# Two chained layers behind clustered attention: the sums and the output products of a step are queued one step later

## The chip, the cores and the metric

The kernel runs on one core of one Trainium2 chip. The metric is the device time of one execution in microseconds (us). The engines named below are PE (matrix products), DVE (vector), ACT (activation), POOL (GpSimd) and SP (which issues the transfers). Each takes its instructions in the order in which they were written for it, and they wait for each other through semaphores.

## The reference

Clustered attention gives 1536 rows of 512 numbers. Two layers follow, and the change lies in them:

```python
def _moe_ref(x, w_in, w_out):                  # first layer, 512 -> 2048 -> 512
    h = x @ w_in
    g = np.maximum(0.01 * h, h)
    return g @ w_out

def _moe2_ref(x, w_in, w_out, a, b):           # second layer, same sizes
    h = x @ w_in
    P = a[0] + a[1] * h + a[2] * h * h + a[3] * h * h * h
    Q = 1.0 + np.abs(b[0]) * np.abs(h) + np.abs(b[1]) * h * h
    g = P / (Q + 1e-06)
    return g @ w_out
```

## The kernel before

**Steps.** Both layers are cut into 112 steps. A step takes one block of tokens (512 in the first layer, 384 in the second) and one slice of 128 of the 2048 hidden numbers. Steps 0 to 47 are the first layer, 48 to 111 the second. Every matrix is split into a high and a low part (names that end in h and l), and a product is three products. PE's part of step i is 12 matmuls for h(i) and then, once the nonlinearity is there, 12 (first layer) or 9 (second) for y(i). The steps of one token block and one group of slices add up in the same y tiles; a group has 4 slices, but the first group of the first layer is cut into two of 2. At the last slice the y tiles are added to an array in SBUF, by three or four DVE operations named acc (`collect`). I call that **the sums of step s** and the change to the next y tiles a **crossing**. There are as many sums of a crossing as y tiles, and each y tile has a single buffer, so that y(s+1), the first of the next block, cannot start in a tile before that tile's sum is done.

**Between h and y.** In the first layer ACT applies the leaky step to h (L1064), ACT casts gh (L1055) and DVE takes gl = h - gh (L1060). In the second layer ACT makes |h| as y (L1071) and u (L1072), POOL makes z in two operations (L1075, L1078), DVE two operations on u (L1079, L1080), ACT the reciprocal r by ln and exp (L1091, L1092), DVE three operations that end in g, written over h (L1093, L1096, L1099), then gh and gl as before. h has four buffers in PSUM.

**Order.** The scheduler is off: what the last loop of the program writes in pass i is the order on every engine. In pass i PE gets h(i) and then y(i-3) (`LAG = 3`); gh and gl have three buffers each. So gh(i) also waits for y(i-3), which reads the buffer that it takes over.

**Weights.** Among these operations stand those that fetch and split the weights of later groups (`weights.step`, the last thing in each pass). In the first layer the weights come as 64-bit numbers and are converted: ACT L818, DVE L825 and L831, then an ACT cast (L838) and a POOL subtraction (L841). In the second layer only the last two are left, one pair in every second step of its first three groups.

Of the kernel before, what the change touches and what calls it, by code (L numbers as in the profile page):

```python
# [30 lines left out]
def clustered_attention_moe_moe2(  # L31
# [103 lines left out]
    def tile_of(x):  # L135
        u, a = divmod(x, T // 2)
        return a * 2 + u

    class Attention:
# [414 lines left out]
        def hi(self, u, part):  # L554
            un = self.unit[u]
            gi, i = divmod(u, QT)
            if i == 0 and part == 0:
                self.group[gi] = {
                    "ph": self.pt.tile([P, T, BLK], F32R, tag="ph", name="ph"),
                    "pl": self.pt.tile([P, T, BLK], F32R, tag="pl", name="pl"),  # L560
                }
            n = T // 2
            un["hi", part] = self.group[gi]["ph"][:, part * n:(part + 1) * n, i * P:(i + 1) * P]
            nc.scalar.copy(un["hi", part], un["pT", part])  # L564

        def lo(self, u, part):
            un = self.unit[u]
            gi, i = divmod(u, QT)
            n = T // 2
            nc.vector.tensor_tensor(  # L570
                self.group[gi]["pl"][:, part * n:(part + 1) * n, i * P:(i + 1) * P],
                un["pT", part], f32(un["hi", part]), op=ALU.subtract,
            )
            if part == 1:
                del self.unit[u]
# [349 lines left out]
    def queue_group(n):  # L925
        for which in ("wi", "wo"):
            if (n, which) in scratch:
                weights.add((which, n), scratch[n, which], which, n % 2, False)
            else:
                weights.add((which, n), weight_source(n, which), which, n % 2, WIDE)  # L930
# [10 lines left out]
    with tc.manual_schedule():  # L941
        wctx = ctx.enter_context(ExitStack())
# [49 lines left out]
        yp = wctx.enter_context(tc.tile_pool(name="yp", bufs=1))  # L992
        x1["c"] = [yp.tile([P, NCT, BLK], F32R, name=nm) for nm in ("xhc", "xlc")]
        accs = yp.tile([P, NCT * NT], F32, name="acc")
        gp_ = wctx.enter_context(tc.tile_pool(name="gp", bufs=3))
        ew = wctx.enter_context(tc.tile_pool(name="ew", bufs=2))
        open_stage("wstb")
        hps = wctx.enter_context(tc.tile_pool(name="hps", bufs=4, space=PSUM))
# [3 lines left out]
            weights.step()  # L1002

        LNC = float(2.0 ** -LN_SHIFT)
        LAG = 3
        steps = [
            (n, j, f) for n, (m, f0, nf) in enumerate(groups)
            for j in range(NT // width(m)) for f in range(nf)
# [2 lines left out]
        NS = len(steps)  # L1011
        st = {}
        cur = {}

        def mm3(o, pairs, first, last):
            n = len(pairs)
            for idx, (l, r) in enumerate(pairs):
                nc.tensor.matmul(  # L1018
                    o, lhsT=l, rhs=r,
                    start=(first and idx == 0), stop=(last and idx == n - 1),  # L1020
                )

        def tl(nm):
            return ew.tile([P, BLK], F32, tag=nm, name=nm)

        def rational(i):
            return groups[steps[i][0]][0] == 1

        def wide(i):
            return width(groups[steps[i][0]][0])  # L1030
# [31 lines left out]
        def leaky(i):  # L1062
            h = st[i]["h"]
            nc.scalar.activation(h, h, AF.Prelu, alpha=0.01)  # L1064
            hi(i)
            lo(i)

        def ratio_act(i):
            d = st[i]
            d["y"], d["z"], d["u"] = tl("y"), tl("z"), tl("u")  # L1070
            nc.scalar.activation(d["y"], d["h"], AF.Abs)  # L1071
            nc.scalar.activation(  # L1072
                d["u"], d["h"], AF.Identity, bias=nav[:, 2:3], scale=nav[:, 3:4]
            )
            nc.gpsimd.tensor_scalar(  # L1075
                d["z"], d["y"], abv[:, 1:2], abv[:, 0:1], op0=ALU.mult, op1=ALU.add
            )
            nc.gpsimd.tensor_tensor(d["z"], d["z"], d["y"], op=ALU.mult)  # L1078
            nc.vector.tensor_tensor(d["u"], d["u"], d["h"], op=ALU.mult)  # L1079
            nc.vector.scalar_tensor_tensor(  # L1080
                d["u"], d["u"], nav[:, 1:2], d["h"], op0=ALU.add, op1=ALU.mult
            )

        def ratio_end(i):
            d = st[i]
            if i < M0 + LAG:
                r = tl("r")
            else:
                r = yps.tile([P, 512], F32, tag="y3", name="r")[:, 0:BLK]
            ln = tl("ln")  # L1090
            nc.scalar.activation(ln, d["z"], AF.Ln, scale=LNC, bias=lnc)  # L1091
            nc.scalar.activation(r, ln, AF.Exp, bias=lnb, scale=-1.0)  # L1092
            nc.vector.scalar_tensor_tensor(  # L1093
                d["u"], d["u"], nav[:, 0:1], r, op0=ALU.add, op1=ALU.mult
            )
            nc.vector.scalar_tensor_tensor(  # L1096
                r, d["z"], 1.000001, r, op0=ALU.add, op1=ALU.mult
            )
            nc.vector.scalar_tensor_tensor(  # L1099
                d["h"], r, -2.0, d["u"], op0=ALU.add, op1=ALU.mult  # L1100
            )

        def start(i):
            if rational(i):
                ratio_act(i)
            else:
                leaky(i)

        def shape(i):
            final = rational(i)  # L1110
            return final, QT if final else NCT, 512

        def back(i):
            n, j, f = steps[i]
            final, NO, NW = shape(i)
            d = st.pop(i)
            gh, gl = d["gh"], d["gl"]
            woh, wol = weights.get(("wo", n))
            for o in range(NO):
                if f == 0:  # L1120
                    cur[o] = yps.tile([P, 512], F32, tag=f"y{o}", name=f"y{o}")
                sl = slice(o * P, (o + 1) * P)
                if final:
                    pairs = [(gh[:, sl], woh[:, f, :]), (gh[:, sl], wol[:, f, :]), (gl[:, sl], woh[:, f, :])]
                else:
                    pairs = [(woh[:, f, sl], gh), (woh[:, f, sl], gl), (wol[:, f, sl], gh)]
                mm3(cur[o][:, 0:NW], pairs, f == 0, f == groups[n][2] - 1)

        def collect(i):
            n, j, f = steps[i]  # L1130
            first = groups[n][1] == 0
            nf = groups[n][2]
            last = groups[n][1] + nf == NG * NF
            final, NO, NW = shape(i)
            if f < nf - 1:
                return
            for o in range(NO):
                a = accs[:, (j * NO + o) * NW:(j * NO + o + 1) * NW]
                if first:
                    nc.vector.tensor_copy(a, cur[o][:, 0:NW])  # L1140
                else:
                    nc.vector.tensor_tensor(a, cur[o][:, 0:NW], a, op=ALU.add)
                if last:
                    if final:
                        b, t = divmod(j * QT + o, T)
                        t = tile_of(t)
                        nc.sync.dma_start(
                            out=out[b * S:(b + 1) * S, :].rearrange("(p t) c -> t p c", t=T)[t],
                            in_=a,
                        )  # L1150
                    else:
                        later.append((j, o, a))
# [9 lines left out]
                    nc.gpsimd.tensor_tensor(l, a[:, b - t0:e - t0], f32(h), op=ALU.subtract)  # L1162

        later = []
        for i in range(NS + LAG):
            if i < NS and steps[i][1:] == (0, 0):
                n1 = steps[i][0] + 1
                begin, total = i, 0
                count = NT // wide(i) * groups[n1 - 1][2]
                if n1 < len(groups):  # L1170
                    queue_group(n1)
                    if WIDE and n1 + NG - 1 > NG0 and n1 + NG - 1 < len(groups):
                        queue_scratch(n1 + NG - 1)
                    total = weights.pending()
            if i < NS:
                make_h(i)
            if i >= LAG:
                back(i - LAG)
            if 0 <= i - 1 < NS:
                start(i - 1)  # L1180
            if 0 <= i - 2 < NS and rational(i - 2):
                hi(i - 2)
                lo(i - 2)
            if later:
                next_x()
            if i >= LAG:
                collect(i - LAG)
            if 0 <= i - 1 < NS and rational(i - 1):
                ratio_end(i - 1)
            due = total * min(i - begin + 1, count - 1) // (count - 1)  # L1190
            weights.step(max(0, due - (total - weights.pending())))
            if i < LAG and weights.waits_for(("wo", 0)):
                weights.step(4)
            if i == LAG - 2:
                while weights.waits_for(("wo", 0)):
                    weights.step()
# [29 lines left out]
```

## Time and profile before

| what | value |
|---|---|
| median of 3 runs | 810.77 us (810.54 to 816.19) |
| the profiled execution, its own time | 810.76 us |
| its span in the trace | 808.9 us |
| PE busy | 790.3 us, 98% of the span |
| DVE, ACT, POOL busy | 655.8, 526.7, 401.5 us |
| first layer, first h to the second layer's first h | 269.29 to 524.82 us |
| second layer, first h to the last sum | 524.82 to 805.81 us |

Matmuls are pipelined, so the busy time of PE says little about small waits. They are seen in the starts: 12 matmuls of a step that start at equal distances are not held up, and a longer distance is a wait.

### The profile page before, as it was taken

The page shows a single profiled execution, that of the slowest core. Times are in us where ns is not written, and L with a number is a line of the kernel's source. Part 1 is how long each engine was busy: PE and PEld are TensorE (multiplying, and loading weights), DVE is VectorE, ACT ScalarE, POOL GpSimd, SP SyncE. Part 2 cuts the span into 40 slices and gives each one's busy share as a digit, 9 for nine tenths or more (in the row PEclk, how much of TensorE's full clock was granted, in tenths as well). Part 3 has the DMA queues.
Part 4 walks back from the last instruction along what each step waited for, and adds up shares of the span by engine and source line. Part 5 has one row for each costly group of instructions (what it writes and reads, how often), then busy time and mean ns, then how long its engine had stood idle before and what let it go on. Part 6 is the DMA issues. An engine that isn't in the chain of part 4 may idle for free.

```text
span 808.9 us, 12601 instructions
## 1 busy us (share of the span) xinstructions
PE 790.3 (98%) x4202; PEld 687.6 (85%) x4202; DVE 655.8 (81%) x1198; ACT 526.7 (65%) x1104; POOL 401.5 (50%) x440
## 2 busy tenths in 40 slices
PE   8899999999999999999999999999999999999997
PEld 5799898999888888888888888899989888988995
DVE  6788998988988678866577478668888888888997
ACT  4689988988899454453344245456676667766763
POOL 3867877877676323230031033267555555554442
PEclk9899999999999999999999999999999999999999
DMA  3783663753420224345446434421001010000112
GB/s 108 179 210 77 154 150 69 183 138 79 98 90 0 105 105 156 104 157 182 145 141 209 149 116 145 158 69 39 28 28 39 27 40 28 27 0 1 40 40 79
DMA packets 42256, 78.71 MB, mean 97 GB/s; under 512 B 5328, under 2 KB 25296, under 8 KB 42192
## 3 DMA queue, kind: packets, MB, share of 16 engines
q1 hardware_dynamic: 41904, 77.83, 32.7%
q8 instruction: 33, 0.54, 0.3%
q14 instruction: 31, 0.25, 0.1%
q10 hardware_dynamic: 288, 0.08, 0.0%
HBM read 49.84 MB, written 9.96 MB: 74 GB/s over the span
## 4 chain that ended last, share of the span: by engine, by line
PE 59%; POOL 14%; DVE 11%; ACT 9%; issue 7%; DMA 0%; POOLq 0%; DVEq 0%; ACTq 0%
PE h L1018 21%; PE y L1018 19%; POOL z L1078 5%; PE o L587 5%; PE s L507 5%; PE pT L551 5%; POOL z L1075 3%; DVE pl L570 3%; DVE nm L516 2%; PE sims L315 2%; POOL wol L841 2%; ACT ln L1091 2%; ACT r L1092 2%; POOL wil L841 2%; ACT ph L564 1%
## 5 line engine op out<-in xcount | busy, mean ns | idle before, releaser
L841 POOL TENSOR_TENSOR wil<-wf,wih 128x512 fp32r<-128x512 f32 x32 | 42.8, 1349 | 148.9 <-ACT wih L838 137.3
L570 DVE TENSOR_TENSOR pl<-pT,ph 128x384 fp32r<-128x384 f32 x192 | 97.2, 546 | 19.6 <-ACT ph L564 19.1
L1055 ACT CAST gh<-h 128x384 fp32r<-128x384 f32 (+1 forms) x112 | 59.0, 526 | 82.5 <-DVE h L1099 51.9
L543 POOL TENSOR_SCALAR e<-e,sum 128x768 f32<-128x768 f32 x96 | 87.9, 928 | 46.0 <-DVE sum L539 31.3
L1060 DVE TENSOR_TENSOR gl<-h,gh 128x384 fp32r<-128x384 f32 (+1 forms) x112 | 68.1, 608 | 40.7 <-ACT gh L1055 40.6
L564 ACT CAST ph<-pT 128x384 fp32r<-128x384 f32 x192 | 82.4, 481 | 17.1 <-PE pT L551 15.5
L1018 PE MATMUL h<-xha,wil 128*128 128x512 f32 (+1 forms) x256 | 93.5, 365 | 0.0
L1018 PE MATMUL h<-xha,wih 128*128 128x512 f32 (+1 forms) x256 | 93.3, 364 | 0.0
L1018 PE MATMUL h<-xla,wih 128*128 128x512 f32 (+1 forms) x256 | 93.3, 364 | 0.0
L516 DVE TENSOR_REDUCE nm<-s 128x1 f32<-128x768 f32 x96 | 90.8, 947 | 2.3 <-PE s L507 1.8
L527 ACT ACTIVATE e<-s,nm 128x768 f32<-128x768 f32 x96 | 87.3, 910 | 5.1 <-DVE sum L539 2.6
L551 PE MATMUL pT<-ident,e 128*128 128x128 f32 x576 | 82.7, 278 | 2.9 <-DVE pl L570 2.6
L831 DVE SCALAR_TENSOR_TENSOR wf<-st,wf 128x512 int32<-128x512 int32 x124 | 82.5, 717 | 0.0
L1075 POOL TENSOR_SCALAR z<-y,abv 128x384 f32<-128x384 f32 x64 | 43.1, 673 | 73.0 <-ACT y L1071 73.0
L1018 PE MATMUL y<-woh,gl 128*128 128x512 f32 x192 | 76.3, 398 | 0.7 <-DVE gl L1060 0.3
L1018 PE MATMUL y<-woh,gh 128*128 128x512 f32 x192 | 76.2, 397 | 0.8 <-ACT gh L1055 0.6
L551 PEld LDWEIGHTS pT<-ident,e 128*128 128x128 f32 x576 | 68.2, 144 | 9.4 <-DVE pl L570 3.6
L1018 PE MATMUL y<-wol,gh 128*128 128x512 f32 x192 | 75.2, 392 | 0.0
L1018 PE MATMUL y<-gh,wol 128*128 128x512 f32 x192 | 75.0, 390 | 0.0
L1018 PE MATMUL y<-gh,woh 128*128 128x512 f32 x192 | 74.8, 390 | 0.0
L1018 PE MATMUL y<-gl,woh 128*128 128x512 f32 x192 | 74.7, 389 | 0.0
L841 POOL TENSOR_TENSOR wol<-wf,woh 128x512 fp32r<-128x512 f32 x32 | 41.8, 1314 | 66.1 <-ACT woh L838 50.2
(125 smaller groups left out, 2044.3 us busy)
## 6 DMA issues: line engine op xcount, KB each, us to landing
st<-in_moe_w_out_dram SPq DMA_DIRECT2D x32, 512.0 KB, 4.4
st<-in_moe_w_in_dram SPq DMA_DIRECT2D x30, 512.0 KB, 4.6
a<-hl SPq DMA_DIRECT2D x56, 192.0 KB, 3.7
b<-hl SPq DMA_DIRECT2D x28, 192.0 KB, 5.9
wf<-scratch_wi SPq DMA_DIRECT2D x14, 256.0 KB, 2.6
qraw<-in_q_dram SPq DMA_DIRECT2D x16, 192.0 KB, 2.7
kraw<-in_k_dram SPq DMA_DIRECT2D x16, 192.0 KB, 3.6
vraw<-in_v_dram SPq DMA_DIRECT2D x8, 384.0 KB, 5.8
```

What stands on the lines that cost most here:

```text
L516: nc.vector.reduce_max(un["nm"], un["s"][:, 0:S], axis=AX.X, negate=True)
L527: nc.scalar.activation(un["e"], un["s"][:, 0:S], AF.Exp, bias=un["nm"], accum_out=un["recip"])
L543: nc.gpsimd.tensor_scalar(un["e"], un["e"], un["recip"], 1.0, op0=ALU.mult, op1=ALU.mult)
L551: nc.tensor.transpose(pp[:, kt * P:(kt + 1) * P], un["e"][:, k0:k0 + P], ident)
L564: nc.scalar.copy(un["hi", part], un["pT", part])
L570: nc.vector.tensor_tensor(self.group[gi]["pl"][:, part * n:(part + 1) * n, i * P:(i + 1) * P], un["pT", part], f32(un["hi", part]), op=ALU ...
L831: nc.vector.scalar_tensor_tensor(wi, hold["st", i][:, :, :, 1 - w], sc, wi, op0=op, op1=ALU.bitwise_or)
L841: nc.gpsimd.tensor_tensor(hold["l"][:, i:i + wr, :], hold["wf", i], f32(hold["h"][:, i:i + wr, :]), op=ALU.subtract,)
L1018: nc.tensor.matmul(o, lhsT=l, rhs=r, start=(first and idx == 0), stop=(last and idx == n - 1),)
L1055: nc.scalar.copy(d["gh"], d["h"])
L1060: nc.vector.tensor_tensor(d["gl"], d["h"], f32(d["gh"]), op=ALU.subtract)
L1075: nc.gpsimd.tensor_scalar(d["z"], d["y"], abv[:, 1:2], abv[:, 0:1], op0=ALU.mult, op1=ALU.add)
```

## The change

In pass i the order becomes: h(i); in the second layer ln and exp of step i-2; the first operations of step i-1; the three DVE operations that end step i-2; the two DVE operations on u of step i-1; the sums of step i-5; gh and gl of step i-2; a piece of the next layer's x if one is due; y(i-4); the weights. LAG is 4 in both layers, gh and gl get a fourth buffer, and `ratio_end` is split in three functions.

```diff
-        gp_ = wctx.enter_context(tc.tile_pool(name="gp", bufs=3))
+        gp_ = wctx.enter_context(tc.tile_pool(name="gp", bufs=4))
...
-        LAG = 3
+        LAG = 4
...
+        def ratio_poly(i):
+            d = st[i]
             nc.vector.tensor_tensor(d["u"], d["u"], d["h"], op=ALU.mult)
...
-        def ratio_end(i):
+        def ratio_recip(i):
             d = st[i]
             if i < M0 + LAG:
                 r = tl("r")
...
+            d["r"] = r
+
+        def ratio_end(i):
+            d = st[i]
+            r = d["r"]
...
-        for i in range(NS + LAG):
+        for i in range(NS + LAG + 1):
...
+            old = 0 <= i - 2 < NS and rational(i - 2)
+            new = 0 <= i - 1 < NS and rational(i - 1)
             if i < NS:
                 make_h(i)
-            if i >= LAG:
-                back(i - LAG)
-            if 0 <= i - 1 < NS:
-                start(i - 1)
-            if 0 <= i - 2 < NS and rational(i - 2):
+            if old:
+                ratio_recip(i - 2)
+            if new:
+                ratio_act(i - 1)
+            elif 0 <= i - 1 < NS:
+                leaky(i - 1)
+            if old:
+                ratio_end(i - 2)
+            if new:
+                ratio_poly(i - 1)
+            if i > LAG:
+                collect(i - LAG - 1)
+            if old:
                 hi(i - 2)
                 lo(i - 2)
             if later:
                 next_x()
-            if i >= LAG:
-                collect(i - LAG)
-            if 0 <= i - 1 < NS and rational(i - 1):
-                ratio_end(i - 1)
+            if LAG <= i < NS + LAG:
+                back(i - LAG)
```

On DVE in the first layer, around gl of steps 8 and 9, the order before, from the sums of step 5 on (acc; the gl rows are those of steps 8 and 9, the wf rows weight conversion):

```order
L1140 COPY acc<-y_4245 128x512
L1140 COPY acc<-y_4249 128x512
L1140 COPY acc<-y_4253 128x512
L1140 COPY acc<-y_4257 128x512
L831 SCALAR_TENSOR_TENSOR wf<-st,wf 128x512 x2
L825 TENSOR_SCALAR wf<-wf 128x512 x2
L1060 TENSOR_TENSOR gl<-h,gh 128x512
L831 SCALAR_TENSOR_TENSOR wf<-st,wf 128x512 x4
L1060 TENSOR_TENSOR gl<-h,gh 128x512
```

The same place after, with the same sums of step 5 at its end:

```order
L831 SCALAR_TENSOR_TENSOR wf<-st,wf 128x512 x2
L825 TENSOR_SCALAR wf<-wf 128x512 x2
L1060 TENSOR_TENSOR gl<-h,gh 128x512
L831 SCALAR_TENSOR_TENSOR wf<-st,wf 128x512 x4
L1060 TENSOR_TENSOR gl<-h,gh 128x512
L1142 COPY acc<-y_4286 128x512
L1142 COPY acc<-y_4290 128x512
L1142 COPY acc<-y_4294 128x512
L1142 COPY acc<-y_4298 128x512
```

The sums of step s stood behind gl(s+2) and now stand behind gl(s+4), and so behind two steps of weight conversion more.

On ACT in the second layer, at a step with a weight cast (L838), before:

```order
L1055 CAST gh<-h 128x384
L1091 ACTIVATE ln<-z,lnc 128x384
L1092 ACTIVATE r<-ln,lnb 128x384
L838 CAST woh<-wf 128x512
L1071 ACTIVATE y<-h 128x384
L1072 ACTIVATE u<-h,nav 128x384
```

and after:

```order
L1055 CAST gh<-h 128x384
L838 CAST woh<-wf 128x512
L1094 ACTIVATE ln<-z,lnc 128x384
L1095 ACTIVATE r<-ln,lnb 128x384
L1071 ACTIVATE y<-h 128x384
L1072 ACTIVATE u<-h,nav 128x384
```

Apart from the cast, ACT's order in the second layer is the same: what moved to the front of a pass stood at the end of the pass before.

On DVE at the end of the program, after:

```order
L1082 TENSOR_TENSOR u<-u,h 128x384
L1083 SCALAR_TENSOR_TENSOR u<-u,nav,h 128x384
L1144 TENSOR_TENSOR acc<-y_8813,acc 128x512
L1144 TENSOR_TENSOR acc<-y_8817,acc 128x512
L1144 TENSOR_TENSOR acc<-y_8821,acc 128x512
L1060 TENSOR_TENSOR gl<-h,gh 128x384
```

The first two rows are of step 111, the last step, and the sums are those of step 107; before, these sums stood two steps earlier, between gl of step 108 and the end operations of step 109.

## Rows read from the trace of the kernel before

**Rows 1.** The page, granted clock of PE in 40 slices (9 is 90% or more).

```profile
PEclk9899999999999999999999999999999999999999
```

**Rows 2.** Timeline of PE, second layer, first matmuls of h (start, length, instruction).

```profile
543.61 0.33 PE L1018 MATMUL h<-xha,wih 128*128 128x384 f32 x1
...
551.98 0.33 PE L1018 MATMUL h<-xha,wih 128*128 128x384 f32 x1
...
581.29 0.33 PE L1018 MATMUL h<-xhc,wih 128*128 128x384 f32 x1
...
729.61 0.34 PE L1018 MATMUL h<-xha,wih 128*128 128x384 f32 x1
...
746.69 0.34 PE L1018 MATMUL h<-xha,wih 128*128 128x384 f32 x1
...
775.90 0.34 PE L1018 MATMUL h<-xhb,wih 128*128 128x384 f32 x1
```

**Rows 3.** Timeline of PE, second layer, two neighbours in y.

```profile
600.49 0.39 PE L1018 MATMUL y<-wol,gh 128*128 128x512 f32 x1
601.00 0.50 PE L1018 MATMUL y<-woh,gl 128*128 128x512 f32 x1
```

**Rows 4.** Timeline of DVE, second layer, the first end operation of three steps.

```profile
579.36 0.61 DVE L1093 SCALAR_TENSOR_TENSOR u<-u,nav,r 128x384 f32<-128x384 f32 x1 [0.28 <-ACT r L1092]
...
584.29 0.61 DVE L1093 SCALAR_TENSOR_TENSOR u<-u,nav,r 128x384 f32<-128x384 f32 x1 [1.68 <-ACT r L1092]
...
587.84 0.61 DVE L1093 SCALAR_TENSOR_TENSOR u<-u,nav,r 128x384 f32<-128x384 f32 x1 [0.29 <-ACT r L1092]
```

**Rows 5.** Timeline of ACT, the ln in between (in brackets: idle before, releaser).

```profile
583.02 0.62 ACT L1091 ACTIVATE ln<-z,lnc 128x384 f32<-128x384 f32 x1 [1.47 <-POOL z L1078]
```

**Rows 6.** Timeline of POOL, same place.

```profile
579.94 1.30 POOL L841 TENSOR_TENSOR wol<-wf,woh 128x512 fp32r<-128x512 f32 x1 [1.89 <-ACT woh L838]
581.23 0.66 POOL L1075 TENSOR_SCALAR z<-y,abv 128x384 f32<-128x384 f32 x1
```

**Rows 7.** Timeline of PE, first layer: first y(0), then first matmuls of h(46), h(47).

```profile
280.48 0.39 PE L1018 MATMUL y<-gh,woh 128*128 128x512 f32 x1
...
513.78 0.39 PE L1018 MATMUL h<-xhb,wih 128*128 128x512 f32 x1
...
519.30 0.39 PE L1018 MATMUL h<-xhb,wih 128*128 128x512 f32 x1
```

**Rows 8.** Timeline of ACT, first layer, gh of step 45.

```profile
514.03 0.59 ACT L1055 CAST gh<-h 128x512 fp32r<-128x512 f32 x1 [0.64 <-PE y L1018]
```

**Rows 9.** Timeline of DVE, first layer, in order of time.

```profile
288.81 2.47 DVE L1140 COPY acc<-y 128x512 f32<-128x512 f32 x4
...
295.98 0.69 DVE L1060 TENSOR_TENSOR gl<-h,gh 128x512 fp32r<-128x512 f32 x1 [0.42 <-ACT gh L1055]
...
311.39 1.28 DVE L831 SCALAR_TENSOR_TENSOR wf<-st,wf 128x512 int32<-128x512 int32 x2
...
321.65 0.69 DVE L1060 TENSOR_TENSOR gl<-h,gh 128x512 fp32r<-128x512 f32 x1 [2.83 <-ACT gh L1055]
...
344.30 2.49 DVE L831 SCALAR_TENSOR_TENSOR wf<-st,wf 128x512 int32<-128x512 int32 x4
...
354.01 0.69 DVE L1060 TENSOR_TENSOR gl<-h,gh 128x512 fp32r<-128x512 f32 x1 [1.20 <-ACT gh L1055]
...
514.65 0.69 DVE L1060 TENSOR_TENSOR gl<-h,gh 128x512 fp32r<-128x512 f32 x1 [0.86 <-ACT gh L1055]
```

**Rows 10.** Timeline of PE at the end: first matmul of y(107).

```profile
790.51 0.40 PE L1018 MATMUL y<-woh,gh 128*128 128x512 f32 x1
```

**Rows 11.** Timeline of ACT at the end: u of step 110.

```profile
791.10 0.67 ACT L1072 ACTIVATE u<-h,nav 128x384 f32<-128x384 f32 x1
```

**Rows 12.** Timeline of DVE at the end: sums of steps 107 and 111.

```profile
791.41 2.08 DVE L1142 TENSOR_TENSOR acc<-y,acc 128x512 f32<-128x512 f32 x3 [0.99 <-PE y L1018]
...
803.73 2.08 DVE L1142 TENSOR_TENSOR acc<-y,acc 128x512 f32<-128x512 f32 x3 [0.59 <-PE y L1018]
```

More of the change, by code (lines that the diff above doesn't have):

```diff
@@ L1101, in ratio_end @@
             )
[L1103 to L1107, printed above, removed]
         def shape(i):
```

## The prediction

> **What bounds the kernel now.** I read the clock first, then the starts of PE's matmuls, then who is late where they are late. PE's clock is granted in full nearly everywhere [rows 1], so no time lies there. In the second layer PE's starts are even for long stretches: from h(100) at 746.69 to h(107) at 775.90 a step takes 4.173 us, and from h(54) to h(61) 4.187 [rows 2], both without a visible gap. A whole layer at that pace has nothing to give but its waits. Between h(52) at 543.61 and h(96) at 729.61, the stretch with weight casts, 44 steps take 186.0 us [rows 2], where 28 steps at 4.187 and 16 at 4.173 (the two paces alternate by group) would take 184.0. So **2.0 us** are waits. One of them is seen: two neighbours in y start 0.51 apart, and the second reads gl [rows 3]; nine of them in half a step would be 0.23 apart.
>
> Why gl is late shows on DVE. From one end operation to the next it takes 3.55 us without a weight cast and 4.93 with one [rows 4]; every second step has one, so the chain of gh, ln, exp and end operations goes at 4.24 us a step and PE at 4.18. The cast itself is not the price: its POOL subtraction takes 1.30, z starts as it ends, and ln then waits 1.47 for z [rows 5, 6]. The chain is slower than PE by 0.06 a step, uses up the three steps of room, and from then on PE waits.
>
> **Part 1, one more step of room in the second layer: -2.0 us.** y(i-4) instead of y(i-3) gives each gl one step of 4.18 us more. The shortfall over the 44 steps is 44 x 0.06 = 2.6 us, less than that, so the waits go even if the chain stays as slow. It won't: the cast now stands before ln, so POOL gets its 1.30 us while ACT does ln (0.62 [rows 5]), an exp of about that length and |h|, and z is not held up; I count this as nothing more, since the room already covers it. Bounds: 0 (the waits come back elsewhere) and -2.0 (there is no more to remove).
>
> **Part 2, the sums in the first layer: +3.4 us.** Here PE shows no wait now, so each new one is a full loss. A crossing after the change: PE has y(s), h(s+5), y(s+1). DVE has gl(s+4), the sums of s, more conversion. gh(s+4) takes over the buffer that y(s) reads, so it starts only when y(s) is through. What that costs is seen at step 45: PE starts the next h at 513.78, right behind the last matmul of y(42); gh waits for it and starts at 514.03, gl ends at 515.34 [rows 7 to 9], 1.56 after. A sum takes 0.68 and four take 2.47 [rows 9], so they start 0.60 apart; the first starts 0.08 before gl's end is recorded and ends at 2.16. PE wants y(s+1) after one h, half of the step of 5.52 [rows 7], or 2.76. So a crossing is free by 0.55 if DVE comes to gl in time.
>
> It doesn't at three of the fourteen crossings inside the layer, all in the first sixteen steps, where groups of two slices bring the sums every second step and two steps of conversion stand between.
> - Step 1. The order up to gl(3) is as before. Before, four sums took DVE from 288.81 and gl(5) ended at 296.67 [rows 9]; without them everything from there is 2.4 earlier, gl(5) ends at 294.27 and the first sum at 294.87. PE has h(4), y(0), h(5), y(1), h(6) from 280.48 [rows 7], 2.5 steps, and wants y(2) at 294.28. Wait **0.6**.
> - Step 5. The sums of step 3 end with the conversion starting 1.48 + 2.39 = 3.87 after y(3). From that first conversion to the end of gl(9) it was 311.39 to 322.34, 10.95 us [rows 9], the same operations as now. First sum ends at 3.87 + 10.95 + 0.60 = 15.42; PE wants y(6) at 13.80. Wait **1.6**.
> - Step 11. The same with 344.30 to 354.70, 10.40 us [rows 9]: 14.87 against 13.80. Wait **1.1**.
>
> With 0.05 of signalling at each this is 3.4. At the other crossings the conversion between has four steps to fit in, and I take the 0.55 as kept. Bounds: 0 (the conversion runs faster, once the sums no longer stand idle before it) and +6.7 (the other eleven each miss by 0.3).
>
> A rule speaks against this part. The Trainium skill, Perfetto Trace Analysis, "Optimizing Tensor Performance", says that independent groups of matmuls should rotate through PSUM banks so that emptying one overlaps the matmuls of the next. The y tiles here don't rotate, and by the rule every crossing would be exposed, which is the second rival below; the trace of before has no PE wait at these crossings, because h stands between, so I go by the rows.
>
> **Part 3, the end: -0.9 us.** The last h is now followed by five y, not four, so it ends one y earlier, 2.09 us. Before, the last h ended one step after y(107) began, 790.51 + 4.17 = 794.68, and the last sum at 805.81 [rows 10, 12]: 11.13 later. After, from the end of h(111): u of step 111 is ready after 1.25 (at step 110, h ends where y(107) starts, 790.51, and u ends at 791.77 [rows 10, 11]), two DVE operations of 0.6 each (their like in [rows 4]) and the first sum of step 107, 0.68, follow, so y(108) starts at 3.1 where PE could have started it at 2.09: a wait of 1.0 that is new. Then y(108) to y(110) take 6.26, and from the start of a y to its last sum it is 2.98 (790.51 to 793.49 [rows 10, 12]). Together 12.34. Less 11.13, less 2.09: -0.9. The sums are through by 4.5 us and step 111 needs one more circle of the chain, 3.55 [rows 4]: 8.1, before y(111) starts at 9.4, so it is covered. Bounds: -1.9 without the new wait, 0 if DVE is a step late.
>
> **Parts at nothing.** The fourth gh and gl buffer costs space only. The first layer's sums are copied into the second layer's x one piece per step; the last piece of the first block comes behind gh(46), 0.25 after y(42), and with gh 0.6 [rows 8], a cast like it and a subtraction like the 1.30 of [rows 6] it is there at 2.8 of the 5.5 us that PE still has until h(48). If that cover went, the second layer would start late by what exceeds it. h(4) now follows h(3) directly and needs gl(0)'s buffer, which is free as y(0) starts. SP's list of transfers is in the same order, and the output goes out behind the last sum as before. One more r lies in SBUF instead of PSUM.
>
> **Sum.** 3.4 - 2.0 - 0.9 = +0.5 on the profiled execution's own 810.76, which stands 0.01 under the median of the runs: **811.3 us**.
>
> **Rivals.**
> 1. The late sums don't come: DVE is ahead, since it no longer stands waiting for y with the conversion behind it. For it: the sums used to hold up the conversion, and the chains of part 2 contain ACT steps that then start earlier. Against: the intervals that I took contain no such wait. Time: 810.76 - 2.9 = 807.9. Chance 0.29.
> 2. Slower: the sums hold up y at every crossing of the first layer, because gh(s+4), gl(s+4) and the first sum stand in a row behind y(s). It decides as soon as gl(s+4) ends later than 2.1 us after y(s). Price: 14 crossings at 1.4, the mean of 1.6 and 1.1, less the 2.9 gained: 810.76 + 19.6 - 2.9 = 827.5. For it: before, gl is often later than that. Against: much of that lateness is the sums' own wait, which goes. Chance 0.09.
> 3. The reordering does nothing in the second layer: DVE meets ln, exp and end in the same circle, and the waits of 2.0 stay since what is late is the chain and not the room. Time 813.3. For it: ACT's and DVE's circles are the same but for the cast and the sums. Against: 2.6 us of shortfall fit into 4.18. Chance 0.08.
>
> **Numbers.** The forecast, 811.3, has 0.50, the three rivals 0.46, and 0.04 is left for things not named. The range goes from rival 1 with the end at its best, 810.76 - 3.9 = 806.9, to the forecast with part 2 at +6.7 and half of part 1, 810.76 + 6.7 - 1.0 - 0.9 = 815.6. One per cent, about what a measurement of this kernel can tell from no change, is 8.1 us: faster than 802.7 needs more than all waits removed (0.02), slower than 818.9 is rival 2 (0.09), within is 0.89.
>
> **What the profile after would show.** Part 1: starts of h(52) to h(96) even, 184 us. Part 2: a larger distance before the first y of steps 2, 6 and 12, with the first sum ending right before it, and none at later crossings. Part 3: one wait of about 1 us before y(108), none later, and 12.3 us from the last h to the last sum. I am wrong if the first layer has no waits, or has them at nearly every crossing.

## The result

The changed kernel is slower: **821.50 us**, the median of seven executions (818.85 to 825.82), against 811.74 for the kernel before in the same comparison. The ratio is **1.0106, 95% interval 1.0082 to 1.0130**. A repetition gave 821.76 us and 1.0106 (1.0087 to 1.0125). The forecast was 811.3 us with a range to 815.6: 0.5 us more than before, where 9.8 were measured. It had the direction right and the size far too small.

The profiled execution of the changed kernel took 821.93 us, its span is 820.1; before, 810.76 and 808.9. The difference of spans, 11.2 us, is made up so. I add, over all matmuls of the two layers, by how much the distance between two starts is longer than 0.231 us (512 columns) or 0.174 (384):

| place | before | after | forecast of the difference |
|---|---|---|---|
| attention, up to the first h | 269.3 | 270.5 | 0 |
| y(2), y(6), y(12) | 0 | 0.70 + 2.07 + 1.23 = 4.0 | +3.4 |
| y(24), y(36), y(44) | 0 | 0.44 + 0.37 + 0.22 = 1.0 | 0 |
| h(4), which now follows h(3) | 0 | 0.2 | 0 |
| y(48), y(52), first crossings of the second layer | 0 | 2.65 + 1.43 = 4.1 | 0 |
| lower clock behind y(6) and y(48) | 0 | 1.5 + 1.5 = 3.0 | 0 |
| other waits from h(52) to h(96) | 2.0 | 0 | -2.0 |
| the end, from the last h to the last sum | 11.1 | 12.4, with one y more behind h (2.1) | -0.9 |

The differences add up to 10.7 of the 11.2 us (the end counts 12.4 - 11.1 - 2.1 = -0.8); the rest is spread over distances below 0.1 us. The 1.2 us of the attention part vary between executions of all these kernels (the first h starts between 269.0 and 271.8 us in the twelve profiles) and are no part of the change.

**The first layer.** The timeline of PE of the changed kernel: the first matmul of y(2), then y(6) with its neighbours, y(12), y(24) and y(36) (start, duration, engine, line, operation, tiles; in brackets the idle time before, and what ended it):

```profile
296.38 0.47 PE L1018 MATMUL y<-gh,woh 128*128 128x512 f32 x1 [0.54 <-DVE acc L1142]
...
318.03 0.39 PE L1018 MATMUL h<-xhb,wil 128*128 128x512 f32 x1
320.33 0.47 PE L1018 MATMUL y<-gh,woh 128*128 128x512 f32 x1 [1.92 <-DVE acc L1142]
320.64 0.53 PE L1018 MATMUL y<-gl,woh 128*128 128x512 f32 x1
320.96 0.63 PE L1018 MATMUL y<-gh,wol 128*128 128x512 f32 x1
321.39 0.63 PE L1018 MATMUL y<-gh,woh 128*128 128x512 f32 x1
...
324.29 0.40 PE L1018 MATMUL y<-gl,woh 128*128 128x512 f32 x1
...
356.38 0.47 PE L1018 MATMUL y<-gh,woh 128*128 128x512 f32 x1 [1.07 <-DVE acc L1144]
...
422.83 0.47 PE L1018 MATMUL y<-gh,woh 128*128 128x512 f32 x1 [0.28 <-DVE acc L1144]
...
489.03 0.47 PE L1018 MATMUL y<-gh,woh 128*128 128x512 f32 x1 [0.20 <-DVE acc L1144]
```

Two things are to be seen. Each of these y waits for DVE's acc, the first sum. And behind the wait of y(6) the matmuls start 0.43 apart instead of 0.23, until 324.29. The DVE rows at y(6) and y(12), which answer to [rows 9] (some line numbers differ by a few from those before):

```profile
314.08 1.88 DVE L831 SCALAR_TENSOR_TENSOR wf<-st,wf 128x512 int32<-128x512 int32 x3
318.90 0.69 DVE L1060 TENSOR_TENSOR gl<-h,gh 128x512 fp32r<-128x512 f32 x1 [2.94 <-ACT gh L1055]
319.51 2.48 DVE L1142 COPY acc<-y 128x512 f32<-128x512 f32 x4
...
354.94 0.69 DVE L1060 TENSOR_TENSOR gl<-h,gh 128x512 fp32r<-128x512 f32 x1 [1.25 <-ACT gh L1055]
355.55 1.88 DVE L1144 TENSOR_TENSOR acc<-y,acc 128x512 f32<-128x512 f32 x3
```

The order is the predicted one: conversion, gl(s+4), sums of s. Before gl, DVE stands idle for 2.94 and 1.25 us behind ACT's gh. The sums could have been taken in that time (PE was through with y(5) as it started h(10), at 315.54), but stood behind gl.

At y(24) gl is later than elsewhere because of ACT. Two rows of ACT there, the changed kernel's and then, from the kernel before, the same cast:

```profile
419.64 0.62 ACT L838 CAST woh<-wf 128x512 fp32r<-128x512 f32 x1 [4.00 <-PE y L1018]
```

```profile
418.30 0.62 ACT L838 CAST woh<-wf 128x512 fp32r<-128x512 f32 x1 [2.66 <-DVE wf L831]
```

After the change this weight cast waits for PE, and the leaky step and gh stand behind it. Before, DVE's conversion was the last that it waited for. It is the same at y(36), where ACT stands idle for 4.08 us.

**The layer change.** DVE and PE of the changed kernel at y(48), then PE at y(52):

```profile
549.75 1.16 DVE L1101 SCALAR_TENSOR_TENSOR u<-u,nav,r 128x384 f32<-128x384 f32 x1 [1.27 <-ACT r L1095]
551.02 0.83 DVE L1104 SCALAR_TENSOR_TENSOR r<-z,r 128x384 f32<-128x384 f32 x1
551.88 1.26 DVE L1107 SCALAR_TENSOR_TENSOR h<-r,u 128x384 f32<-128x384 f32 x1
553.06 0.54 DVE L1082 TENSOR_TENSOR u<-u,h 128x384 f32<-128x384 f32 x1
553.63 0.61 DVE L1083 SCALAR_TENSOR_TENSOR u<-u,nav,h 128x384 f32<-128x384 f32 x1
554.17 2.48 DVE L1144 TENSOR_TENSOR acc<-y,acc 128x512 f32<-128x512 f32 x4
```

```profile
552.18 0.34 PE L1018 MATMUL h<-xha,wil 128*128 128x384 f32 x1
554.90 0.50 PE L1018 MATMUL y<-woh,gh 128*128 128x512 f32 x1 [2.39 <-DVE acc L1144]
...
574.60 0.50 PE L1018 MATMUL y<-woh,gh 128*128 128x512 f32 x1 [1.15 <-DVE acc L1142]
...
580.97 0.33 PE L1018 MATMUL h<-xhb,wih 128*128 128x384 f32 x1
...
739.86 0.34 PE L1018 MATMUL h<-xha,wih 128*128 128x384 f32 x1
```

y(47) was through at 550.25, but its sums stand behind five operations of the chain, three that end step 50 and two on u of step 51, and the first of these waits for r until 549.75. PE could have started y(48) at 552.35.

The last two rows are h(58) and h(96): 38 steps in 158.89 us. That is 4.181 a step, and no start in between is late by 0.1 us. Before, 44 steps from h(52) to h(96) lost 2.0 us [rows 2].

**The clock.** A table of stretches of the changed kernel (stretch; its length; busy time of PE, PE's weight loads, DVE, ACT and POOL; then the granted clock of PE, the share of DMA and its GB/s). The page's own row of the clock, which answers to [rows 1] and stands first here, does not show the falls in its slices of 20 us:

```profile
PEclk9799999999999999999999999999999999999999
```

```profile
311.00:318.00 7.00, 7.00 (x32) 5.82 (x31) 4.94 (x7) 4.08 (x8) 3.41 (x4) 1.00 0.55 180
318.00:320.40 2.40, 0.48 (x3) 0.10 (x1) 1.50 (x3) 0.84 (x2) 0.80 (x1) 1.00 0.72 280
320.40:324.40 4.00, 4.00 (x11) 3.17 (x12) 4.00 (x9) 0.00 (x0) 0.00 (x0) 0.57 0.02 4
324.40:331.00 6.60, 6.60 (x31) 5.39 (x30) 1.35 (x3) 3.38 (x7) 2.55 (x2) 1.00 0.50 159
...
552.30:554.90 2.60, 0.22 (x2) 0.00 (x0) 2.56 (x5) 0.49 (x2) 0.42 (x1) 1.00 0.06 24
556.20:559.80 3.60, 3.60 (x12) 3.20 (x11) 3.45 (x6) 1.51 (x3) 2.60 (x3) 0.53 0.03 7
```

After each of the two longest waits the engine runs near the lower of its two levels, 1.2 GHz (0.50), for some 4 us, and loses about 1.5 us each time.

**The end.** PE at y(108) and the DVE rows that answer to [rows 12]:

```profile
806.40 0.39 PE L1018 MATMUL y<-woh,gl 128*128 128x512 f32 x1
807.79 0.47 PE L1018 MATMUL y<-woh,gh 128*128 128x512 f32 x1 [1.00 <-ACT ln L1094]
```

```profile
806.96 1.88 DVE L1144 TENSOR_TENSOR acc<-y,acc 128x512 f32<-128x512 f32 x3
...
814.91 2.05 DVE L1144 TENSOR_TENSOR acc<-y,acc 128x512 f32<-128x512 f32 x3 [2.86 <-PE y L1018]
```

y(108) starts as the first sum of step 107 is done; the trace names ACT's ln, but that was long over. The wait is 1.16 us. The last h ends at 804.54, the last sum at 816.96: 12.42 later, where the prediction said 12.34.

### The profile page after: what moved, and what is told of

It is laid out like the page before. It is cut to its first block, busy times and chain, and to the rows that moved or that the text cites. A ratio compares the mean times of both kernels' runs of the same rounds, so it can differ in the third digit from the quotient of the medians.

```text
span 820.1 us, 12602 instructions
## 1 busy us (share of the span) xinstructions
PE 794.6 (97%) x4202; PEld 691.2 (84%) x4202; DVE 651.7 (79%) x1198; ACT 529.4 (65%) x1104; POOL 399.6 (49%) x440
## 4 chain that ended last, share of the span: by engine, by line
PE 71%; DVE 14%; ACT 7%; issue 4%; POOL 2%; DMA 1%; POOLq 0%; SPq 0%; DVEq 0%; ACTq 0%
PE y L1018 28%; PE h L1018 25%; PE o L587 5%; PE s L507 5%; PE pT L551 5%; DVE pl L570 3%; DVE nm L516 2%; PE sims L315 2%; ACT ph L564 1%; ACT e L527 1%; ACT gh L1055 1%; DVE acc L1144 1%; DVE wf L831 1%; DVE h L1107 1%; PE pa L238 1%
## 5 line engine op out<-in xcount | busy, mean ns | idle before, releaser
L831 DVE SCALAR_TENSOR_TENSOR wf<-st,wf 128x512 int32<-128x512 int32 x124 | 80.5, 703 | 0.0
```

The source lines that it names most:

```text
L831: nc.vector.scalar_tensor_tensor(wi, hold["st", i][:, :, :, 1 - w], sc, wi, op0=op, op1=ALU.bitwise_or)
```

## The experiments

The theory: PE loses its time at crossings, since the sums of step s now stand on DVE behind work that is itself late (gl(s+4) in the first layer, the end of step s+3 and the poly of s+4 in the second), and the clock adds to the long ones. The room of four steps by itself costs nothing. The rivals are named in the expectations.

**The room alone.** The kernel before, with this and nothing else:

```diff
-        gp_ = wctx.enter_context(tc.tile_pool(name="gp", bufs=3))
+        gp_ = wctx.enter_context(tc.tile_pool(name="gp", bufs=4))
-        LAG = 3
+        LAG = 4
```

> Only the room of four steps and the fourth gh and gl buffer; order of second layer, place of the sums as before. Theory (the loss is the sums queued behind gl(s+4), and what follows from it, the lag is a gain): the first layer has no waits, since the sums of step s stand behind gl(s+3), whose buffer y(s-1) has left; the 2.0 us between h(52) and h(96) go; the end gives about 0.9: 808 to 809 us, ratio 0.996 to 0.998. Rival A (the fourth buffers and the lag cost by themselves, by address or by waits for buffers): above 814. Rival B (the reordering of the second layer, not the room, took the 2.0 us away): 811 to 812, with the waits between h(52) and h(96) still there.

Measured: 812.02 us, ratio to before 0.9993 (0.9982 to 1.0004). So rival A falls: the buffers and the lag cost nothing. The forecast gain did not come either; time and waits are those of rival B, though not at the same places. The waits for gl are gone and others have taken their place, 0.1 to 0.65 us at each of the eleven crossings from y(52) to y(92), 2.5 us together. The largest, PE at y(56) and then DVE:

```profile
578.88 0.34 PE L1018 MATMUL h<-xhc,wil 128*128 128x384 f32 x1
579.71 0.47 PE L1018 MATMUL y<-woh,gh 128*128 128x512 f32 x1 [0.49 <-DVE acc L1140]
```

```profile
578.41 0.55 DVE L1060 TENSOR_TENSOR gl<-h,gh 128x384 fp32r<-128x384 f32 x1
578.88 1.88 DVE L1140 COPY acc<-y 128x512 f32<-128x512 f32 x3
```

In this order the sums of s stand behind gl(s+2). The chain, slower than PE, falls back until the sums behind it hold PE: gl(73) ends 14.1 us after its h began and the first sum takes about 0.6 more, just when PE wants y(72), three and a half steps (14.65 us) after that h began. More room for gl only moved the wait to the sums.

**All sums first in the pass.** The changed kernel, with one call moved:

```diff
             if i < NS:
                 make_h(i)
+            if i > LAG:
+                collect(i - LAG - 1)
             if old:
                 ratio_recip(i - 2)
...
-            if i > LAG:
-                collect(i - LAG - 1)
             if old:
                 hi(i - 2)
```

> The change with the sums of y put first in each pass, ahead of gl(s+4) in the first layer and ahead of end and poly in the second. Theory: all waits of 0.4 us and more at y(2), y(6), y(12), y(24), y(36) go, and with them the fall of the clock behind y(6); y(48) and y(52) wait below 0.3, the clock behind y(48) stays full; y(108) waits below 0.5: 807 to 809 us. Rival A (fourth buffers and lag): above 814, waits still there. Rival C (the chain of the second layer is late at the layer change because of the new order there, and not because of the sums): first layer free, y(48) still waits 2 us or more with the clock falling: 811 to 814.

Measured: **808.74 us, ratio to before 0.9957 (0.9942 to 0.9971)**, 12.8 us less than the change's 821.50 (in ratios to the kernel before, 0.9957 against 1.0106). All waits of PE from y(2) to y(108) are gone; 0.35 is left at y(111), behind gh. DVE and PE at y(6) of this kernel, then DVE and PE at y(52):

```profile
315.25 2.47 DVE L1142 COPY acc<-y 128x512 f32<-128x512 f32 x4
318.22 0.69 DVE L1060 TENSOR_TENSOR gl<-h,gh 128x512 fp32r<-128x512 f32 x1 [0.50 <-ACT gh L1055]
...
560.87 1.88 DVE L1142 COPY acc<-y 128x512 f32<-128x512 f32 x3
```

```profile
561.70 0.33 PE L1018 MATMUL h<-xhb,wil 128*128 128x384 f32 x1
561.87 0.39 PE L1018 MATMUL y<-woh,gh 128*128 128x512 f32 x1
```

The sums fill the time in which DVE would otherwise stand before gl, and y(52) follows h without a gap. The clock is 1.00 in the stretches 310 to 330 and 540 to 570. Theory holds; rivals A and C fall.

**Only the first layer's sums first.** As above, but `collect` stands first only for steps of the first layer, the 47th included; the others stay behind the end and poly operations.

```diff
+            if i > LAG and not rational(i - LAG - 1):
+                collect(i - LAG - 1)
...
-            if i > LAG:
+            if i > LAG and rational(i - LAG - 1):
                 collect(i - LAG - 1)
```

> The change with only the first layer's sums (up to those of step 47) put first in each pass; those of the second layer stay behind end and poly. Theory: the first layer and y(48) as with all sums early; y(52) may keep its 1.3 us and y(108) its 1.2: 809 to 811 us, 1 to 2.5 more than with all sums early. Rival C: y(48) still waits 2 us or more: 812 to 815. Rival A: above 816.

Measured: 815.11 us, ratio to before 1.0036 (1.0024 to 1.0048), 6.4 above the version with all sums first. The first layer and y(48) are free, as the theory has it; the size was missed. y(52), which had waited 1.3 in the change, now waits 3.77, and 2.7 of lower clock follow:

```profile
561.92 0.34 PE L1018 MATMUL h<-xhb,wil 128*128 128x384 f32 x1
565.86 0.79 PE L1018 MATMUL y<-woh,gh 128*128 128x512 f32 x1 [3.60 <-DVE acc L1142]
566.46 0.63 PE L1018 MATMUL y<-wol,gh 128*128 128x512 f32 x1
```

```profile
562.42 0.61 DVE L1101 SCALAR_TENSOR_TENSOR u<-u,nav,r 128x384 f32<-128x384 f32 x1 [1.24 <-ACT r L1095]
...
565.12 1.88 DVE L1142 COPY acc<-y 128x512 f32<-128x512 f32 x3
```

PE wants y(52) at 562.1. DVE starts the end of step 54 only at 562.42, and has five operations to do before the first sum. So the debt of the chain is paid at the first crossings, at y(48) and y(52) in the change (2.65 and 1.43), at y(52) alone here: as PE stands, the chain catches up (gl ends 13.8 us after the end of its h at step 54, 7 to 9 from step 57 on), and later crossings cost nothing, but for y(108), which keeps its 1.16.

**The new order without the room.** All sums first, but `LAG = 3` and three buffers for gh and gl:

```diff
-        gp_ = wctx.enter_context(tc.tile_pool(name="gp", bufs=4))
+        gp_ = wctx.enter_context(tc.tile_pool(name="gp", bufs=3))
-        LAG = 4
+        LAG = 3
```

> All sums first in each pass, the new order of the second layer, but room of three steps and three gh and gl buffers as before. Theory (the room took the 2.0 us away): the waits between h(52) and h(96) come back to 1 to 2 us, the end loses the 0.9, first layer free: 810 to 812 us. Rival B (the order took them away): no waits there, 808 to 810, the same as with room of four.

Measured: 810.51 us, ratio to before 0.9969 (0.9956 to 0.9983). One wait is left between h(52) and h(96), 0.78 at y(52). The time lies in the range of the theory, not of rival B, but the waits side with rival B: the new order takes nearly all waits of the second layer away without more room. gl ends 11.6 us after the end of its h at step 61 and 10.3 at step 73, where it was 12.65 and 12.8 before: the chain is no longer slower than PE. The early sums are not needed for that: in the change, with its late sums, gl of step 73 ends 7.1 after its h. Which move of the new order does it, the cast ahead of ln or another, was not tested. The room adds the end's gain and y(52): 0.9957 (0.9942 to 0.9971) against 0.9969, intervals that overlap.

**Only the first layer's sums late.** The counterpart: sums up to step 43 as in the change, all later ones first.

```diff
+            early = i - LAG - 1 >= 47
+            if early:
+                collect(i - LAG - 1)
...
-            if i > LAG:
+            if i > LAG and not early:
                 collect(i - LAG - 1)
```

> The counterpart: sums of the first layer up to step 43 behind gl(s+4) as in the change, those of step 47 and of the second layer first in the pass. Theory: the waits of the change's first layer come back as they were, 4.0 us at y(2), y(6), y(12), 0.8 at y(24) and y(36), 1.4 of lower clock behind y(6): 6.2 more than the 808.7 with all sums early, 814 to 816 us. The second layer starts with its chain as late as the sums of step 43 make it, and may lose up to 2 us more at y(50) to y(52): at most 817. Rival (the first layer's waits and the second layer's were not additive, or the waits of the first layer are not from the sums): below 812.

Measured: 815.62 us, ratio to before 1.0034 (1.0016 to 1.0053). The waits are those of the change to 0.02: 0.68, 2.07, 1.23, 0.44, 0.36, with 0.4 at y(52). What did not come back in the profiled execution (812.95 us) is the clock:

```profile
316.60:318.90 2.30, 0.39 (x2) 0.03 (x1) 1.43 (x3) 0.80 (x2) 0.77 (x1) 1.00 0.78 292
318.90:322.90 4.00, 4.00 (x18) 3.31 (x19) 4.00 (x8) 0.00 (x0) 0.00 (x0) 1.00 0.01 4
```

The same wait, at the same place, and full clock behind it. The ten executions of this kernel fall into four of 812.7 to 813.8 us and six of 815.5 to 816.8. That the clock makes this difference is likely, but not shown: the mean granted clock was 0.993 to 0.995 in the four and 0.989 to 0.992 in the six, yet the kernel before, without such waits, spreads as well (810.4 at 0.996 to 813.6 at 0.989 in the same comparison).

**r in PSUM two steps sooner.** All sums first, and

```diff
-            if i < M0 + LAG:
+            if i < M0 + LAG - 2:
                 r = tl("r")
```

> All sums early, and r of steps 50 and 51 in PSUM instead of SBUF. Theory (the end operations with r in SBUF are slow beside POOL's work, 1.25 to 1.7 us against 0.6, and make the chain late at the layer change, but PE no longer waits there): the three end operations of steps 50 and 51 take 0.6 each, gl(50) and gl(51) come 2 us or more earlier than the 11.9 and 12.2 after their h; the time stays at 808.7 within 0.8. Rival (the SBUF place has no part in it): these operations stay at 1.2 us and more, and gl(50), gl(51) stay at 12.

Measured: 808.34 us, ratio to before 0.9949 (0.9934 to 0.9965), the fastest of all here, though not told apart from 0.9957. The operations became short: the last of step 51 took 1.27 with r in SBUF and 0.57 with r in PSUM. At step 50 it had been 0.57 in SBUF too. gl(51) came only 0.6 earlier and gl(50) 0.6 later, so the expectation of 2 us was wrong. The r of step 50, now in the place of the fourth y tile, has a wait of its own: ACT stands 4.51 us before it, until DVE's sums of step 47 are done. So r's place in SBUF is not what makes the chain late at the layer change. It is as late in the kernel before (gl(49) 11.9 us after its h); only nothing waited for it there.

**The clock by itself.** All sums first, and ahead of the sums of steps 15, 23, 31 and 39 copies of y whose results nobody uses:

```diff
+            for _ in range({15: 5, 23: 6, 31: 7, 39: 9}.get(i, 0)):
+                nc.vector.tensor_copy(tl("r"), cur[NO - 1][:, 0:BLK])
             for o in range(NO):
```

> All sums early, and ahead of the sums of steps 15, 23, 31 and 39 five, six, seven and nine idle copies of y on DVE (results unused), so that PE waits before y(16), y(24), y(32), y(40) for about 0.7, 1.3, 1.8 and 2.9 us, with 44 us of steady matmuls between. Theory (the clock falls behind a wait of 2 us and more, not behind one of 1.3 and less): behind the longest the granted clock is near 0.55 for some 4 us, and the matmuls lose 1.4 to 1.7 us; behind the two shortest none; the third, between the 1.3 and the 2.07 seen, tells where. Rival (the falls belong to the places, groups of two slices and the layer change, not to the length of the wait): full clock behind all four.

Measured, in one execution of 812.91 us: waits of 0.56, 1.10, 1.49 and 2.42 us, and full clock behind all four, the longest included. The theory is wrong, and the forecast is the rival's. But the place alone does not explain it either: behind the 2.07 at y(6) the clock fell in the change and, in the profiled execution with only the first layer's sums late, did not. Therefore the change once more, and longer waits twice.

> The change unaltered, a second profile. Theory: the waits of PE are the same to 0.05 us in the same places (0.70, 2.07, 1.23 in the first layer, 2.55 at y(48), 1.3 at y(52), 1.16 at y(108)), since they come from the order on DVE. What is open is the clock: with all sums early a wait of 2.07 at the same place had full clock behind it. If the fall hangs on the place and its wait alone, both falls (0.57 and 0.53) are there again; if it comes and goes from run to run, one or both are missing, and the executions spread over 3 us or more, those with more mean clock being the shorter ones. Time 818.5 to 823, ratio 1.008 to 1.013.

Measured: 821.76 us, ratio 1.0106 (1.0087 to 1.0125). Waits of 0.69, 2.07, 1.23, 2.53, 1.30 and 1.16, and both falls again, 0.57 and 0.53.

```diff
-            for _ in range({15: 5, 23: 6, 31: 7, 39: 9}.get(i, 0)):
+            for _ in range({15: 8, 23: 9, 31: 10, 39: 11}.get(i, 0)):
```

> As the kernel with idle copies ahead of the sums of steps 15, 23, 31 and 39, now eight, nine, ten and eleven of them, for waits before y(16), y(24), y(32), y(40) of about 2.0, 2.4, 2.9 and 3.4 us (measured steps were 0.56, 1.10, 1.49 and 2.42 for five, six, seven and nine). If a long wait lowers the clock by its length, the longer ones show 0.5 to 0.6 behind them for some 4 us and the shorter do not; if chance has a part in it, the order is mixed. Time: 808.7 plus the waits, 10.7, is 819.4, plus 1.5 for each fall, up to 825.

> The same kernel with eight to eleven copies, profiled once more. If the length of the wait alone decides, the same waits have the same clock behind them; if not, another selection of the four.

Measured: 823.87 us, ratio to before 1.0153 (1.0124 to 1.0182), and 823.73 us in the second profile. The waits are 1.96, 2.49, 2.89 and 3.35 us in both. In the first profile the clock fell behind the second, third and fourth of them, in the second behind the second and third (0.58 and 0.61), and behind the longest, 516.0 to 519.5, it did not. The first fence is of the first profile, the other of the second:

```profile
374.00:378.00 4.00, 3.94 (x17) 3.29 (x18) 3.81 (x8) 0.85 (x2) 0.00 (x0) 1.00 0.02 4
...
421.70:425.70 4.00, 4.00 (x12) 3.15 (x11) 3.18 (x7) 0.58 (x1) 0.00 (x0) 0.57 0.00 0
...
517.80:521.80 4.00, 3.91 (x11) 3.19 (x12) 3.61 (x7) 2.25 (x4) 1.29 (x1) 0.62 0.01 2
```

```profile
516.00:519.50 3.50, 0.33 (x2) 0.01 (x1) 3.50 (x8) 0.09 (x1) 0.00 (x0) 1.00 0.45 179
519.50:523.50 4.00, 3.98 (x17) 3.29 (x18) 3.79 (x8) 3.03 (x6) 1.30 (x1) 1.00 0.01 2
```

So the length does not decide alone. Nor does the place: here the clock fell at crossings where only the idle copies made PE wait. What else decides stays open. Over these two layers in all profiles, waits up to 1.96 us were never followed by the fall, and those from 2.07 to 3.77 in 10 of 13 cases.

## Why the prediction was wrong

- **Part 2, the three crossings, was right in place and cause, and near in size**: 0.6, 1.6 and 1.1 forecast (3.4 with signalling), 0.70, 2.07 and 1.23 seen, 4.0 together. Rival 1, that late sums don't come, falls.
- **Part 2, the other eleven crossings**, was a term mis-sized. It took them "as kept" free by 0.55. Two miss by 0.44 and 0.37, y(24) and y(36), and y(44) by 0.22. At the first two gl comes late, since ACT stands idle 4.0 us before a weight cast that waits for PE, and gh is behind it. The likely reason, read from the order and not tested by itself: the last y of the old group, which reads the weights to be overwritten, is a step later with the room of four. The prediction's upper bound of 6.7 covered this 1.0.
- **The step that failed is "Parts at nothing"**, in what it says of the layer change: it looked at the x of the second layer and not at the sums of the last first-layer step, which the change puts behind the end of step 50. It counted no wait of y(48), which lost 2.65 us. The same holds for the crossing after it, 1.43. Most of the price could have been read from the rows of before. h(60) ends at 581.29 - 2.09 = 579.20 [rows 2], and its first end operation starts at 587.84 [rows 4], 8.6 us later. After the change PE wants y(s+1) two steps, 8.4 us, after the end of h(s+3), so it stands until that end, a poly (2.7 us together, 562.42 to 565.12 above; by the 0.6 each of [rows 4], 3.0) and a sum (0.7) are done: 8.6 + 2.7 + 0.7 - 8.4 = 3.6 us, an estimate, to be paid at one crossing after another until the chain has caught up. Measured were 3.77 where y(52) bore it alone, and 2.65 and 1.43 in the change. Part 3 worked this out for y(108) only, where the chain had long caught up, and was right there (1.0 forecast, 1.16 seen). Also at nothing stood h(4), which lost 0.2: it now stands ahead of y(0), and starts at 281.80, right behind the end of gl(0) at 281.75.
- **Lower clock, 3.0 us, was no term at all.** The prediction read that the clock is full [rows 1] and did not ask whether it stays so behind the waits that it forecast. Behind a wait of its own figure, 1.6, no fall was seen in any run; y(6) measured 2.07. The 3.0 us are those of the profiled execution, and probably vary from one to the next: of the change's seven, the two with a mean granted clock of 0.995 and 0.996 took 818.96 and 818.85 us, where three at 0.987 took 821.5 to 822.1.
- **Part 1 had the right amount for the wrong reason.** The 2.0 us went, but by the order and not by the room: the room alone gives 0.9993 (0.9982 to 1.0004), the order with early sums 0.9969 (0.9956 to 0.9983). That the amount came out is luck. "The room already covers it" overlooked that the sums stand behind the chain as well. Rival 3 fails in its forecast, since the waits went, but its reason, that the chain is late and not the room too small, is what the room alone shows.
- **Part 3** was right: 12.34 us from the last h to the last sum forecast, 12.42 seen.
- **Rival 2**, each of fourteen crossings at 1.4, fails as well: five lose more than 0.3. The rule of the Trainium skill behind it (Perfetto Trace Analysis, "Optimizing Tensor Performance", on rotating through PSUM banks) points at the right weakness: every wait of 0.3 us and more in the change is PE standing before a y tile that is not yet emptied. With the sums first the same single tiles cost nothing.

With these the sum is 4.0 + 1.0 + 0.2 + 4.1 + 3.0 - 2.0 - 0.8 = 9.5, against 9.8 between the medians.

## What to carry to other kernels

Where an accumulator has one buffer, the operation that empties it is the most urgent on its engine: put it ahead of work that itself waits; here it fitted into time in which the engine would have stood idle. Before such an operation is queued one step later, walk every crossing, the first ones of a new stage above all, and ask how late the work is that now stands ahead of it; a lateness that nothing waits for in the old order has a price in the new. If predicted waits of PE reach about 2 us, allow for a fall of the clock behind them: here it came behind 10 of 13.

## What the runs showed of the hardware

- Behind 10 of 13 waits of 2.07 to 3.77 us PE's granted clock fell from full to a mean of 0.50 to 0.62 over stretches of some 4 us (5 in one case), at 1.4 to 2.7 us each, and behind none of up to 1.96. The same wait of 2.07 had it twice and not the third time, and one of 3.35 once in two executions of one kernel. The Trainium skill, TensorE: Matmul & The Clock Gate, Part 1, says of the rise of the clock at a kernel's start that its point varies from run to run; the rows here show such a variation for the fall.
- DVE's last end operation (L1107) took 1.25 to 1.26 us in all four steps of the change with r in SBUF, and 0.57 with r in PSUM. With the sums first it took 0.83, 0.92, 0.57 and 1.27 with r in SBUF, so what runs beside it counts: the 0.57 (545.14 to 545.71) fell into a time in which POOL stood idle (542.82 to 546.50), and the other three ran beside POOL's operations on z. The Trainium skill, SBUF — State Buffer, "Who interferes with whom", says that a DVE instruction with two SBUF inputs contends with a POOL instruction that reads SBUF; r and u are such inputs here, and these rows agree.
